# Attention and feed-forward kernel: deeper staging of the weights, 32 halves decoded in 24 units, one more chunk with fp32 value products, feed-forward work from unit 24 on

## The chip, the cores and the metric

The kernel runs on one core of one Trainium2 chip. The metric is the device time of one execution in microseconds (us); of several runs the median is taken. TensorE is called PE here, VectorE DVE, ScalarE ACT, GpSimd POOL and SyncE SP, as in the profile.

## The reference

Attention over 4 batches, 8 heads, 576 positions and head size 64, with a bias from a small network on the distance of two positions, then a layer norm and a feed-forward block of 16 x 128 hidden channels:

```python
scores = scale * np.matmul(q, k.transpose(0, 1, 3, 2))
x = (psi_rel / psi_i)[..., None]
h = np.maximum(x @ w1 + b1, 0.0)
bias = h @ w2
scores = scores + bias.transpose(2, 0, 1)[None, :, :, :]
attn = np.exp(scores - max); attn = attn / (sum + 1e-09)
out = np.matmul(attn, v)
...
xn = (x - mu) / np.sqrt(var + 1e-06) * g_ln
ch = np.maximum(xn @ w_ch1, 0.0) @ w_ch2
return x + ch
```

The feed-forward weights `w_ch1` and `w_ch2` arrive as 64-bit floats, seen by the kernel as pairs of 32-bit words.

## The kernel before, in words

The attention runs in 144 units `(b, c, h)`: batch `b`, a chunk `c` of 128 query rows (chunk 4 is the tail of 64 rows, where a unit takes two heads), head `h`. `ORD` gives the order of the pairs `(b, c)`; units 0 to 7 are the tails of batches 0 and 1, units 8 to 15 chunk 0 of batch 0, 16 to 23 chunk 0 of batch 1, 24 to 39 chunk 0 of batches 2 and 3, 40 to 47 the other two tails, and units of 8 follow to 143. For each unit PE multiplies q and k (`qk`, L390), DVE adds the bias and takes the row maximum (`softmax1`, L414), ACT takes the exponential (L418).

What follows has two forms. Pairs in `NAT` keep fp32: PE transposes the probabilities (`softmax2`, L436 and L437), ACT copies them (L438, L439), and PE multiplies by fp32 v (L486, L503 for the tails). The others split the probabilities into two fp16 parts, on ACT (L423) and DVE (L442, L444), a DMA transposes them (L447, 1152 columns), and PE multiplies by v that is split in two as well (`pv_mms`, L457). For these batches v is measured (`v_max`, L341), the result goes out to DRAM and comes back broadcast (`vall`, reduced at L350), and `split_v` splits it (L365, L368). `uv[b]` is the first unit of batch `b` in the second form; it sets when these steps of the batch are placed.

The feed-forward weights are 32 halves `(f, i)` of 512 KB. `load_w` issues a half on SP's queue into one of two staging buffers (the two slots of `wend`); `decode_w` makes fp32 of it with three DVE instructions (L602, L604, L606), PE adds up a Gram matrix of it (L615), and after 8 halves `w_scale` finds a scale and `split_w` splits each half into fp16 high and low parts (ACT L641, DVE L644) into the slot below. One half is decoded per unit in the program, and each decode is followed by the load of the next half. After a group of 8 halves is split, feed-forward work with it can run: `ffn_micro` does one step, `ffn_w1` (48 matmuls, L667, then ACT L672 and DVE L675 to `hh`) or `ffn_w2` (12 matmuls, L695, into `y`, added to x by DVE L706). There are 144 such steps; a budget `mbank` lets at most two run per unit.

Bias rows are made in 36 groups (`bias_relu`, `bias_mm`), stored to DRAM (`nb`) and loaded skewed, one load per head and chunk (`ldb`), on SP's queue. K, q and v come on POOL's queue. Seven bias groups stand ahead of unit 0; DMAs in `gate` wait for one of them. The program text isn't the last word on order: a scheduler puts each engine's instructions in an order by its own estimate of times, and the engines then run in that order.

Of the kernel before, what the change touches and what calls it, by code (L numbers as in the profile page):

```python
# [22 lines left out]
def kernel(  # L23
# [83 lines left out]
    wslot = [wp.tile([128, 1024], F32, name=f"w{f}") for f in range(NF - 1)]  # L107
# [71 lines left out]
    def bias_mm(gi):  # L179
# [17 lines left out]
        else:  # L197
# [37 lines left out]
    gend = {c: sum(len(range(8 * x, min(36, 8 * x + 8))) for x in corder[:corder.index(c) + 1])  # L235
            for c in range(5)}

    NAT = {(0, 4), (1, 4), (0, 0)}

    def nat_pv(b, c):  # L240
        return (b, c) in NAT

    uv = {}
    for u, (b, c, h) in enumerate(units):
# [4 lines left out]
    seg = []  # L249
    for n, (b, c) in enumerate(ORD):  # L250
        seg.append(seg[-1] + (ORD[n - 1][1] != c) if n else 0)
    loads = []
    for n, (b, c) in enumerate(ORD):
        u0 = ustart[b, c]
        for g in range(4):
            if n == 0 or ORD[n - 1][0] != b:
                loads.append((u0 + (g if c == 4 else 2 * g) - 4, "k", (n, b, g)))
        for hh in range(2 if c < 4 else 1):
            loads.append((u0 + 4 * hh - 3, "q", (b, c, hh)))
        if n == 0 or ORD[n - 1][1] != c:  # L260
            for h in range(NH if c < 4 else 4):
# [11 lines left out]
    gate, gate_on = [], [True]  # L273
# [294 lines left out]

        defer(lo)

    wraw = {}

    def load_w(f, i):
        if f < NF - 2:
            dst = wslot[NF - 1 + i]
        elif f == NF - 2 and i == 1:
            dst = wslot[NF]
        else:
            dst = [ep.tile([128, EW], F32, tag="e", name="wst")[:, 0:512] for _ in range(2)]
            for j in range(2):  # L580
                ld = SY.dma_start(
                    out=dst[j].bitcast(U32),
                    in_=w_ch[f].bitcast(U32)[:, 1024 * i + 512 * j:1024 * i + 512 * j + 512])
                after(ld, ttri[max(ttri)])
            wraw[f, i] = dst
            return
        ld = SY.dma_start(out=dst.bitcast(U32), in_=w_ch[f].bitcast(U32)[:, 1024 * i:1024 * i + 1024])
        if gate_on[0]:
            gate.append((ld, 1 + 2 * i))
        if f >= NF - 2:  # L590
            after(ld, ttri[max(ttri)])
        wraw[f, i] = dst

    def decode_w(f, i):
        wf = wslot[f + 1][:, 512 * i:512 * i + 512]
        src = wraw.pop((f, i))
        src = src if isinstance(src, list) else [src]
        nw = 512 // len(src)
        for j, raw in enumerate(src):
            raw = raw.bitcast(U32).rearrange("p (a b) -> p a b", b=2)  # L600
            w = wslot[f + 1][:, 512 * i + nw * j:512 * i + nw * j + nw].bitcast(U32)
            V.tensor_scalar(out=w, in0=raw[:, :, 1], scalar1=3, scalar2=0x3FFFFFFF,  # L602
                            op0=ALU.logical_shift_left, op1=ALU.bitwise_and)
            V.scalar_tensor_tensor(out=w, in0=raw[:, :, 0], scalar=29, in1=w,  # L604
                                   op0=ALU.logical_shift_right, op1=ALU.bitwise_or)
            V.scalar_tensor_tensor(out=w, in0=raw[:, :, 1], scalar=0xC0000000, in1=w,  # L606
                                   op0=ALU.bitwise_and, op1=ALU.bitwise_or)
        g = GOF[f]
        f0, f1 = GROUPS[g]
        if g not in gram:  # L610
            gram[g] = ps_y.tile([128, 512], F32, tag="y1", name="gram")
        wb = wf.bitcast(BF16).rearrange("p (a b) -> p a b", b=2)[:, :, 1]
        for c in range(4):
            blk = wb[:, 128 * c:128 * c + 128]
            T.matmul(out=gram[g][:, 128 * i:128 * i + 128], lhsT=blk, rhs=blk,  # L615
                     start=(f == f0 and i == 0 and c == 0), stop=(f == f1 - 1 and i == 1 and c == 3))
# [104 lines left out]
    avail_at = []  # L721

    def next_fs(u):
        if not cur_job:
            navail = sum(1 for a in avail_at if a <= u)
            for j in jobs:
                k, g = j
                if blocks[k][-1] < navail and wready_at.get(g, 1 << 30) <= u:
                    jobs.remove(j)
                    nf = 4 // len(blocks[k])  # L730
                    f0, f1 = GROUPS[g]
                    cur_job.extend((k, range(f, f + nf)) for f in range(f0, f1, nf))
                    break
        return cur_job.pop(0) if cur_job else None
# [34 lines left out]
    gate.append((SY.dma_start(out=gs_sb, in_=g_r), 3))  # L769
    wload = [(f, i) for f in range(NF) for i in range(2)]  # L770
    wdec = list(wload)
    for _ in range(2):
        load_w(*wload.pop(0))
    issue_loads(-6)
    V.memset(mhalf, -0.5)
    V.memset(one_sb, 1.0)
    V.memset(half2, 0.5)
    bias_setup()
    issue_loads(-4)
    NP = 7  # L780
# [41 lines left out]
    u = 0  # L822
    while u < NU + 6 or jobs or cur_job or pend or yq:
        if u >= NEARLY:
            ffn_y()
        softmax1(u)
        issue_loads(u)
        softmax2(u - 1)
        flush()
        for _ in range(8):  # L830
            if wdec and 32 - len(wdec) < 1 + (100 * u) // 100:
                f, i = wdec.pop(0)
                decode_w(f, i)
                if i == 1 and f + 1 == GROUPS[GOF[f]][1]:
                    w_scale(GOF[f])
                if wload:
                    load_w(*wload.pop(0))
        while mm_done[0] < ngroup:
            bias_mm(gorder[mm_done[0]])
            mm_done[0] += 1  # L840
        if u % 2:
            qk(u + 1)
            qk(u + 2)
        while npv <= u - LAG:
            if pv(npv):
                lnq.append([u, len(avail_at) + len(lnq)])
            npv += 1
        for fn in todo.pop(u, []):
            fn()
        for g, (f0, f1) in enumerate(GROUPS):  # L850
            if wdone[0] >= 2 * f1 and g not in wready_at:
                wready_at[g] = u
        if u < NU + 9:
            nav = len([a for a in avail_at if a <= u])
            goal = sum(2 * NF * len(bl) // 4 for bl in blocks if bl[-1] < nav)
            nxt = min((steps_av[bl[-1]] for bl in blocks if bl[-1] >= nav), default=NU + 9)
            mbank += max(0.0, (goal - (ntot - nmicro) - mbank)) / max(1, nxt - u)
            mbank = min(mbank, 2.0)
        else:
            mbank = 1.0  # L860
        flush_lo()
        ffn_y()
        while mbank >= 1.0:
            if not ffn_micro(u):
                break
            mbank -= 1.0
            nmicro -= 1
            if mbank >= 1.0:
                ffn_y()
        bneed = NP + 1 + u if u < 8 else 12  # L870
        for c in (1, 2, 3):
            bneed = max(bneed, gend[c] - 8 + min(8, (u - cfirst[c] + 30) * 8 // 26))
        if ngroup < min(36, bneed):
            bias_relu(gorder[ngroup], 1)
            ngroup += 1
        for _ in range(2):
            if wspl:
                split_w(*wspl.pop(0))
        for it in list(lnq):
            if it[0] == u - 1:  # L880
                ln1(it[1])
# [57 lines left out]
```

## Time and profile before

| what | value |
|---|---|
| median of 3 runs | 746.67 us (737.48, 746.67, 750.48) |
| the profiled execution's own time | 743.11 us |
| its span | 741.3 us, so 1.8 us lie outside |
| busy: PE, DVE, ACT, POOL | 651.0, 489.6, 380.9, 87.0 us |
| mean granted clock of PE | 0.929 of full speed |
| moved by DMA | 123.30 MB |

Busy time is the time in which an engine had an instruction running. An average over the span hides that stages have different limits, so the rows below are taken by stage. The first row of each stage is the unit whose L414 begins it.

### The profile page before, as it was taken

The numbers are of one execution on the slowest core, as the hardware profiler recorded it, in microseconds if no ns is written. First come the engines' busy times: TensorE is split into PE (matmuls) and PEld (weight loads), VectorE is DVE, ScalarE is ACT, GpSimd is POOL, SyncE is SP. The second block draws the span as 40 slices with busy tenths as digits, with TensorE's granted clock in tenths as the row PEclk, the third lists the DMA queues.
The fourth block names the chain that finished last, engine by engine and source line by source line (L and its number), as shares of the span: only waits on it lengthen the run. The fifth ranks groups of instructions, "written<-read, shape, count | busy, mean of one in ns | idle before, by whom it ended". The sixth has DMA issues, their size and how long they took to land. (4 is left out here: it accounts for less than half of the span.)

```text
span 741.3 us, 19318 instructions
## 1 busy us (share of the span) xinstructions
PE 651.0 (88%) x7980; PEld 445.9 (60%) x7980; DVE 489.6 (66%) x1114; ACT 380.9 (51%) x731; POOL 87.0 (12%) x160
## 2 busy tenths in 40 slices
PE   4368887576669999999988969999998999999997
PEld 3134465444456766766755647667666767676774
DVE  4467789987788657766585746575675666767322
ACT  4255874453257555556475735566765445454110
POOL 3301120100110010101110101011001101000000
PEclk9668997658969999999999989999999999999999
DMA  7987977699627688977768799686859777646100
GB/s 258 362 241 224 342 239 194 144 234 202 148 61 144 119 154 206 220 153 174 172 107 159 141 191 187 144 178 152 165 118 238 194 150 159 110 81 126 31 16 15
DMA packets 200909, 123.30 MB, mean 166 GB/s; under 512 B 175860, under 2 KB 176116, under 8 KB 200820
## 3 DMA queue, kind: packets, MB, share of 16 engines
q1 hardware_dynamic: 190676, 88.32, 57.0%
q0 software_dynamic: 9280, 33.56, 14.9%
q8 instruction: 63, 1.03, 0.6%
q10 hardware_dynamic: 864, 0.18, 0.2%
q14 instruction: 26, 0.21, 0.1%
HBM read 63.92 MB, written 15.64 MB: 107 GB/s over the span
## 5 line engine op out<-in xcount | busy, mean ns | idle before, releaser
L667 PE MATMUL hps<-xT,w 128*128 128x128 f16 x3240 | 207.1, 225 | 6.9 <-DVE hh L675 3.8
L667 PEld LDWEIGHTS <-w 128*128 128x128 f16 x3240 | 192.4, 101 | 20.2 <-issue 10.2
L418 ACT ACTIVATE t<-t,m 128x576 f32<-128x576 f32 x144 | 111.0, 771 | 179.2 <-DVE m L414 177.7
L695 PE MATMUL y<-w,hh 128*128 128x512 f16 x810 | 190.8, 384 | 1.5 <-DVE x L706 0.8
L442 DVE SCALAR_TENSOR_TENSOR e<-t,e 128x512 f16<-128x512 f32 x128 | 88.2, 689 | 71.4 <-ACT e L423 71.0
L695 PEld LDWEIGHTS <-hh 128*128 128x128 f16 x864 | 80.4, 99 | 89.4 <-issue 4.9
L414 DVE CUSTOM_DVE_ANT_0 t<-sps,ldb 128x576 f32<-128x576 f32 x144 | 107.1, 753 | 25.5 <-PE sps L390 17.4
L390 PE MATMUL sps<-kf,qf 64*128 64x288 f32 (+1 forms) x640 | 104.9, 468 | 8.0 <-DVE m L414 7.8
L457 PE MATMUL xps<-v,pt 128*128 128x64 f16 (+1 forms) x1904 | 79.7, 198 | 31.1 <-DMA pt<-e 26.3
L457 PEld LDWEIGHTS <-pt 128*128 128x128 f16 (+1 forms) x1904 | 66.3, 102 | 64.5 <-issue 32.8
L423 ACT ACTIVATE e<-t 128x576 f16<-128x576 f32 x128 | 86.3, 679 | 12.0 <-DMA pt<-e 9.3
L706 DVE SCALAR_TENSOR_TENSOR x<-y,ycs,x 128x512 f32<-128x512 f32 x72 | 53.9, 749 | 48.3 <-PE y L695 48.1
L672 ACT ACTIVATE hh<-hps 128x512 f16<-128x512 f32 x72 | 42.1, 584 | 69.2 <-PE hps L667 69.2
L390 PEld LDWEIGHTS sps<-kf,qf 64*128 64x128 f32 (+1 forms) x640 | 49.2, 187 | 42.3 <-issue 12.6
L675 DVE SCALAR_TENSOR_TENSOR hh<-hps,hh 128x512 f16<-128x512 f32 x72 | 49.4, 687 | 35.5 <-ACT hh L672 35.1
L291 POOL DMA_DIRECT2D kf<-in_k_s_dram x64 | 36.0, 562 | 262.6 <-PE sps L390 237.8
L172 ACT ACTIVATE r<-psi_sb,pr_sb 128x512 f32<-128x512 f32 (+31 forms) x92 | 52.7, 633 | 6.4 <-DVE pr_sb L123 3.7
L210 PE MATMUL bps<-r,nw_sb 128*32 128x296 f32 (+34 forms) x474 | 34.1, 368 | 11.3 <-DVE r L174 9.9
L602 DVE TENSOR_SCALAR w<-wend 128x512 uint32<-128x512 uint32 x28 | 12.1, 431 | 34.7 <-DMA wend<-in_w_ch_dram 34.7
L304 POOL DMA_DIRECT2D qf<-in_q_main_dram x32 | 17.6, 551 | 120.2 <-PE sps L390 80.0
L210 PEld LDWEIGHTS bps<-r,nw_sb 128*32 128x32 f32 x474 | 16.7, 118 | 21.8 <-issue 10.4
L641 ACT ACTIVATE w<-w,ws 128x512 f16<-128x512 f32 x28 | 19.7, 716 | 17.7 <-DVE ws L113 9.8
(102 smaller groups left out, 548.0 us busy)
## 6 DMA issues: line engine op xcount, KB each, us to landing
kf<-in_k_s_dram POOLq DMA_DIRECT2D x64, 288.0 KB, 4.4
wend<-in_w_ch_dram SPq DMA_DIRECT2D x29, 512.0 KB, 5.7
nb<-ev SPq DMA_DIRECT2D x33, 296.0 KB, 3.6
ldb<-nb SPq DMA_DIRECT2D x32, 288.0 KB, 5.3
qf<-in_q_main_dram POOLq DMA_DIRECT2D x32, 256.0 KB, 4.7
vf<-in_v_p_dram POOLq DMA_DIRECT2D x16, 320.0 KB, 8.0
out_dram<-x SPq DMA_DIRECT2D x18, 256.0 KB, 2.8
ldb<-nb SPq DMA_DIRECT2D x16, 144.0 KB, 8.2
```

The lines of the kernel that those rows point to most:

```text
L172: S.activation(r[:, 0:n], psi_sb[:, 0:n], AF.Relu, bias=pr_sb[:, g4:g4 + 1], scale=1.0)
L210: T.matmul(out=ps[32 * s:32 * s + 32, hf, a - lo:b - lo], lhsT=nw2_sb, rhs=src, start=True, stop=True)
L390: T.matmul(out=o, lhsT=l, rhs=kk, start=True, stop=True, tile_position=(64 * hf, 64 * e))
L414: ttri[u] = V.tensor_tensor_reduce(out=halves(t), in0=ps[:, :, 0:HS], in1=halves(bias), scale=-0.125, scalar=3e38, op0=ALU.add, op1=ALU.mi ...
L418: S.activation(t, t, AF.Exp, bias=m, scale=-1.0, accum_out=l8[b, c][:, h:h + 1])
L423: S.activation(e16[:, 0:SEQ], t, AF.Copy, scale=E_SCALE)
L442: V.scalar_tensor_tensor(out=e16[:, 640:1152], in0=t[:, 0:512], scalar=E_SCALE, in1=e16[:, 0:512], op0=ALU.mult, op1=ALU.subtract)
L457: T.matmul(out=o, lhsT=p[:, m], rhs=v[:, j, a, :], start=(i == 0), stop=(i == len(ops) - 1))
L667: T.matmul(out=h[:, idx * n:idx * n + n], lhsT=w[:, wo + kk * 128:wo + kk * 128 + 128], rhs=xT[k][:, xo + kk, 0:n], start=(i == 0), stop=( ...
L675: V.scalar_tensor_tensor(out=hh[:, 1], in0=h, scalar=0.0, in1=hh[:, 0], op0=ALU.max, op1=ALU.subtract)
L695: T.matmul(out=yps[k][t], lhsT=hh[:, a, o:o + 128], rhs=w[:, wo:wo + 512], start=(f == f0 and i == 0), stop=(f == f1 - 1 and i == 2))
L706: V.scalar_tensor_tensor(out=x, in0=y, scalar=ycs[:, g:g + 1], in1=x, op0=ALU.mult, op1=ALU.add)
```

## The change

Chunk 0 of batch 1 joins `NAT` and is placed ahead of chunk 0 of batch 0. It thus follows the tail of batch 1, whose k is still there: 60 loads of k are issued where there were 64. Units 0 to 23 are then all in the first form, `nat_end` is 24, and `next_fs` starts no feed-forward job in a unit before 24. `uv[1]` moves from unit 16 to unit 64, so v of batch 1 is split late. A half may be staged in any slot that is free, up to six ahead of the decodes; the slots run out towards the end, the last slots staging one half at a time, and the last two halves go through buffers of the pool `e`. The pace in the program is 4 halves in 3 units, from 1 per unit, and a decode and a later load are made to follow the unit's L414.

```diff
-    ORD = [(0, 4), (1, 4), (0, 0), (1, 0), (2, 0), (3, 0), (3, 4), (2, 4),
+    ORD = [(0, 4), (1, 4), (1, 0), (0, 0), (2, 0), (3, 0), (3, 4), (2, 4),
...
-    NAT = {(0, 4), (1, 4), (0, 0)}
+    NAT = {(0, 4), (1, 4), (1, 0), (0, 0)}
...
+    nat_end = max(u for u, (b, c, h) in enumerate(units) if nat_pv(b, c)) + 1
...
-    def load_w(f, i):
-        if f < NF - 2:
-            dst = wslot[NF - 1 + i]
-        elif f == NF - 2 and i == 1:
-            dst = wslot[NF]
+    wraw, decoded = {}, set()
+    stg = {}
+    def load_w():
+        f, i = wload[0]
+        n = 2 * f + i
+        busy = {x for m, x in stg.items() if m not in decoded}
+        fit = [x for x in range(NF + 1) if x not in busy and (2 * x >= n + 3 or x == 0 and n < 6)]
+        if n < 2 * NF - 2:
+            if not fit or n >= len(decoded) + 6:
+                return False
+            stg[n] = fit[0]
+            dst = wslot[fit[0]]
         else:
+            if n >= len(decoded) + 2:
+                return False
             dst = [ep.tile([128, EW], F32, tag="e", name="wst")[:, 0:512] for _ in range(2)]
...
+            if gate_on[0]:
+                gate.append((ld, min(NP - 1, n + 1)))
+            else:
                 after(ld, ttri[max(ttri)])
...
+            if ttri:
+                after(dec, ttri[max(ttri)])
...
     def next_fs(u):
+        if u < nat_end:
+            return None
...
-    for _ in range(2):
-        load_w(*wload.pop(0))
+    NP = 7
+    while load_w():
+        pass
...
-            if wdec and 32 - len(wdec) < 1 + (100 * u) // 100:
+            if wdec and 32 - len(wdec) < 1 + (4 * u) // 3:
...
-                if wload:
-                    load_w(*wload.pop(0))
+                while wload and load_w():
+                    pass
```

On SP's queue, ahead of the first bias load of unit 0 (`ldb`), three loads of weight halves (`in_w_ch_dram`) stand between the stores of bias groups (`nb`) before:

```order
L220 DMA nb4_133<-ev_238 16x8x592
L587 DMA wend_153<-in_w_ch_dram 128x1024
L220 DMA nb4_133<-rp_262 16x8x592
L220 DMA nb4_133<-ev_286 16x8x592
L769 DMA gs_sb_119<-in_g_r_dram 128x512
L587 DMA wend_153<-in_w_ch_dram 128x1024
L220 DMA nb4_133<-ev_310 16x8x592
L220 DMA nb0_129<-rp_334 16x8x592
L220 DMA nb0_129<-ev_358 16x8x592
L587 DMA wend_153<-in_w_ch_dram 128x1024
L220 DMA nb0_129<-rp_374 16x8x592
L326 DMA ldb_384<-nb4_133 64x576
```

The same stretch of SP's queue after the change, from the second weight load on (one more stands ahead of these rows):

```order
L594 DMA w2_140<-in_w_ch_dram 128x1024
L220 DMA nb4_133<-ev_290 16x8x592
L783 DMA gs_sb_119<-in_g_r_dram 128x512
L594 DMA w3_141<-in_w_ch_dram 128x1024
L220 DMA nb4_133<-ev_314 16x8x592
L594 DMA w4_142<-in_w_ch_dram 128x1024
L220 DMA nb0_129<-rp_338 16x8x592
L594 DMA w5_143<-in_w_ch_dram 128x1024
L220 DMA nb0_129<-ev_362 16x8x592
L594 DMA w6_144<-in_w_ch_dram 128x1024
L220 DMA nb0_129<-rp_378 16x8x592
L328 DMA ldb_388<-nb4_133 64x576
```

Six weight loads now stand ahead of the first bias load, where three did, and they go to six different slots.

DVE at unit 20 before (L442 and L444 make the low fp16 part of the probabilities, L368 that of v, L341 measures v, L675 makes `hh`, L604 is the second decode instruction, always out of `wend`):

```order
L442 SCALAR_TENSOR_TENSOR e_1420<-t,e_1420 128x512
L444 SCALAR_TENSOR_TENSOR e_1420<-t,e_1420 128x64
L368 SCALAR_TENSOR_TENSOR v<-vf,vs,v 128x10x64
L113 TENSOR_SCALAR vs<-var 128x4
L414 ISA t,m<-sps,ldb 128x576
L414 ISA m 128x1
L341 TENSOR_REDUCE vam<-vf 128x1
L675 SCALAR_TENSOR_TENSOR hh<-hps,hh 128x512
L604 SCALAR_TENSOR_TENSOR w_147<-wend,w_147 128x512
L442 SCALAR_TENSOR_TENSOR e_1461<-t,e_1461 128x512
L444 SCALAR_TENSOR_TENSOR e_1461<-t,e_1461 128x64
```

DVE around the same unit after the change (L612, L616 and L618 are the three decode instructions, now out of slots `w_149` to `w_152`):

```order
L416 ISA t,m<-sps,ldb 128x576
L416 ISA m 128x1
L612 TENSOR_SCALAR w_147<-w_149 128x512
L612 TENSOR_SCALAR w_147<-w_150 128x512
L612 TENSOR_SCALAR w_148<-w_151 128x512
L612 TENSOR_SCALAR w_148<-w_152 128x512
L416 ISA t,m<-sps,ldb 128x576
L416 ISA m 128x1
L112 TENSOR_SCALAR var<-var 128x4
L616 SCALAR_TENSOR_TENSOR w_147<-w_149,w_147 128x512
L616 SCALAR_TENSOR_TENSOR w_147<-w_150,w_147 128x512
```

The splitting of the probabilities and the feed-forward work are gone from these units, and four halves are begun together, each out of a buffer of its own.

## Rows read from the trace of the kernel before

**Rows 1.** Windows: busy us of each engine, granted clock, DMA share, GB/s.
```profile
20.00:42.30 22.30, 6.01 (x56) 2.54 (x52) 11.05 (x23) 4.20 (x6) 5.96 (x11) 0.60 1.02 350
42.30:85.70 43.40, 35.63 (x443) 20.87 (x443) 30.85 (x72) 29.25 (x59) 5.20 (x9) 0.85 0.81 250
85.70:149.40 63.70, 47.80 (x397) 32.88 (x395) 56.84 (x128) 38.34 (x80) 11.13 (x21) 0.82 0.75 211
149.40:218.00 68.60, 46.20 (x460) 31.81 (x461) 54.98 (x130) 28.94 (x51) 8.19 (x11) 0.72 0.75 167
218.00:294.80 76.80, 76.80 (x1048) 51.76 (x1047) 52.44 (x122) 45.83 (x85) 6.23 (x11) 0.99 0.75 147
...
80.00:100.00 20.00, 16.33 (x181) 11.13 (x178) 16.48 (x39) 16.29 (x36) 3.04 (x6) 1.00 0.91 323
...
370.00:380.00 10.00, 7.29 (x87) 4.98 (x83) 8.96 (x20) 7.47 (x14) 1.38 (x3) 1.00 0.48 92
```

**Rows 2.** Timeline of DVE: L414 of units 0, 8, 24, 32 and 48.
```profile
42.33 0.76 DVE L414 CUSTOM_DVE_ANT_0 t<-sps,ldb 128x576 f32<-128x576 f32 x1 [0.95 <-DMA ldb<-nb]
...
85.72 0.75 DVE L414 CUSTOM_DVE_ANT_0 t<-sps,ldb 128x576 f32<-128x576 f32 x1
...
149.38 0.75 DVE L414 CUSTOM_DVE_ANT_0 t<-sps,ldb 128x576 f32<-128x576 f32 x1
...
218.01 0.75 DVE L414 CUSTOM_DVE_ANT_0 t<-sps,ldb 128x576 f32<-128x576 f32 x1
...
294.82 0.76 DVE L414 CUSTOM_DVE_ANT_0 t<-sps,ldb 128x576 f32<-128x576 f32 x1 [0.37 <-DMA ldb<-nb]
```

**Rows 3.** Waits of DVE from 42.3, from 149.4, from 350: us, times, longest.
```profile
DVE w L602 <- DMA wend<-in_w_ch_dram: 15.7, 7, 5.3
...
DVE w L602 <- DMA wend<-in_w_ch_dram: 8.5, 6, 2.3
DVE x L706 <- PE y L695: 4.3, 2, 2.3
...
DVE var L350 <- DMA vall<-vmx: 4.4, 1, 4.4
```

**Rows 4.** The chain that ended last: two steps of feed-forward work.
```profile
696.80 2.68 PE hps L667 x48
699.48 2.59 PE y L695 x12
```

**Rows 5.** DMA issues by line: KB each, median us from issue to landing.
```profile
wend<-in_w_ch_dram SPq DMA_DIRECT2D x29, 512.0 KB, 5.7
```

**Rows 6.** Groups of instructions on DVE, whole span: count, busy us, mean ns.
```profile
L442 DVE SCALAR_TENSOR_TENSOR e<-t,e 128x512 f16<-128x512 f32 x128 | 88.2, 689 | 71.4 <-ACT e L423 71.0
...
L706 DVE SCALAR_TENSOR_TENSOR x<-y,ycs,x 128x512 f32<-128x512 f32 x72 | 53.9, 749 | 48.3 <-PE y L695 48.1
...
L675 DVE SCALAR_TENSOR_TENSOR hh<-hps,hh 128x512 f16<-128x512 f32 x72 | 49.4, 687 | 35.5 <-ACT hh L672 35.1
...
L444 DVE SCALAR_TENSOR_TENSOR e<-t,e 128x64 f16<-128x64 f32 x128 | 28.0, 218 | 0.0
...
L604 DVE SCALAR_TENSOR_TENSOR w<-wend,w 128x512 uint32<-128x512 uint32 x28 | 19.2, 687 | 0.2
L606 DVE SCALAR_TENSOR_TENSOR w<-wend,w 128x512 uint32<-128x512 uint32 x28 | 19.2, 687 | 0.2
...
L368 DVE SCALAR_TENSOR_TENSOR v<-vf,vs,v 128x640 f16<-128x640 f32 x16 | 14.0, 874 | 0.2 <-ACT v L365 0.2
...
L341 DVE TENSOR_REDUCE vam<-vf 128x1 f32<-128x640 f32 x16 | 12.5, 811 | 0.0
...
L602 DVE TENSOR_SCALAR w<-wend 128x512 uint32<-128x512 uint32 x28 | 12.1, 431 | 34.7 <-DMA wend<-in_w_ch_dram 34.7
```

**Rows 7.** Timeline of PE in units 8 to 15: transposes, three units apart.
```profile
95.22 0.66 PE L436 MATMUL ptm<-id_sb,t 128*128 128x128 f32 x4
...
103.42 0.66 PE L436 MATMUL ptm<-id_sb,t 128*128 128x128 f32 x4
```

More of the change, by code (lines that the diff above doesn't have):

```diff
@@ L569, in ln2 @@
         defer(lo)
-    wraw = {}
-    def load_w(f, i):
-        if f < NF - 2:
-            dst = wslot[NF - 1 + i]
-        elif f == NF - 2 and i == 1:
-            dst = wslot[NF]
-        else:
+    wraw, decoded = {}, set()
[10 more added lines that the diff above has]
+            dst = wslot[fit[0]]
+        else:
+            if n >= len(decoded) + 2:
+                return False
             dst = [ep.tile([128, EW], F32, tag="e", name="wst")[:, 0:512] for _ in range(2)]
[L580 to L583, printed above, removed]
-                after(ld, ttri[max(ttri)])
[L585 to L591, printed above, removed]
+        wload.pop(0)
+        for j, d in enumerate(dst if isinstance(dst, list) else [dst]):
+            w = d.shape[1]
+            ld = SY.dma_start(out=d.bitcast(U32),
+                              in_=w_ch[f].bitcast(U32)[:, 1024 * i + w * j:1024 * i + w * j + w])
+            if gate_on[0]:
+                gate.append((ld, min(NP - 1, n + 1)))
+            else:
+                after(ld, ttri[max(ttri)])
         wraw[f, i] = dst
+        return True
     def decode_w(f, i):
@@ L596, in decode_w @@
         src = wraw.pop((f, i))
+        decoded.add(2 * f + i)
         src = src if isinstance(src, list) else [src]
@@ L601, in decode_w @@
             w = wslot[f + 1][:, 512 * i + nw * j:512 * i + nw * j + nw].bitcast(U32)
-            V.tensor_scalar(out=w, in0=raw[:, :, 1], scalar1=3, scalar2=0x3FFFFFFF,
-                            op0=ALU.logical_shift_left, op1=ALU.bitwise_and)
+            dec = V.tensor_scalar(out=w, in0=raw[:, :, 1], scalar1=3, scalar2=0x3FFFFFFF,
+                                  op0=ALU.logical_shift_left, op1=ALU.bitwise_and)
+            if ttri:
+                after(dec, ttri[max(ttri)])
             V.scalar_tensor_tensor(out=w, in0=raw[:, :, 0], scalar=29, in1=w,
@@ L779 @@
     issue_loads(-4)
-    NP = 7
     for n in range(NP + 1):
```

## The prediction

> **What bounds the kernel now.** I read the windows by stage first [rows 1]. From 218 us on PE is busy without a gap (76.80 of 76.80 us, granted clock 0.99); what PE has left to do then sets the end. Ahead of that it isn't: from 149.4 to 218.0 PE is busy for 46.20 of 68.60 us at a clock of 0.72, while DVE is busy for 54.98. The marks by unit [rows 2] give the stages: unit 0 begins on DVE at 42.33, unit 8 at 85.72, unit 24 at 149.38, unit 32 at 218.01, unit 48 at 294.82. So the question is when DVE reaches unit 32, and how much feed-forward work PE then owes.
>
> From unit 0 to unit 32 175.7 us go by. DVE is busy in 30.85 + 56.84 + 54.98 = 142.7 of them [rows 1] and idle in 33.0. The waits name the largest cause [rows 3]: the first decode instruction stands for a weight half that has not landed, 15.7 us up to 149.4 and 8.5 us from there to 218. That is 24.2 us; DVE runs in order, so the next L414 is behind each of these waits. The other 8.8 us have several causes, 4.3 of them a wait for y of PE.
>
> **The start.** Unit 0 waits for its bias rows (0.95 us idle until ldb landed) [rows 2]. From 20 to 42.3 us the DMA engines are full: share 1.02 at 350 GB/s [rows 1]. Three more weight halves of 512 KB [rows 5] now stand ahead of those rows on SP's queue; at 350 GB/s one takes 1.5 us, three 4.5 us. Four loads of v move ahead of two of k on POOL's queue as well, which I bound at two more us in the same full stretch and at nothing if they fall behind. I take 4.5: unit 0 at 46.8 us, bounds 42.3 and 48.8.
>
> The Trainium skill says in DMA: Bandwidth & Descriptors, section Issuing engines are not separate DMA queues, that transfers from SP, ACT and POOL end up on the same 16 engines and interleave, so that another queue saves only issue time. By that rule POOL's extra loads count like SP's, and unit 0 would begin at 48.8 and the end come 2 us later than my sum; the share of 1.02 agrees with a common limit, but no row shows what lies ahead of what.
>
> **DVE's work up to unit 32.** I counted the instructions between the L414 of unit 0 and that of unit 32 in both orders and priced the differences [rows 6]. A whole decode is 0.431 + 0.687 + 0.687 = 1.81 us: 30 stand there now, 26 before (before, three were done ahead of unit 0, now none): +7.2. Two half-sized decodes fewer, at half of that each: -1.8. Two more L341 of 0.811: +1.6. Four L368 of 0.874 move to units past 60: -3.5. Eight splits of probabilities go (0.689 + 0.218): -7.3. One hh (0.687) and two y (0.749) fewer: -2.2. The sum is -6.0: 136.7 us of DVE work in place of 142.7. So most of the gain can't come from less work, it must come from the waits.
>
> **The waits for weights.** With up to six halves ahead and one decode per 136.7/32 = 4.3 us of DVE work, a half is asked for some 26 us ahead; landing takes 5.7 us in the median [rows 5]. That leaves nothing of the waits as long as slots are free. They run out for halves 28 and 29, which use one slot in turn: in DVE's order 16 and 8 instructions lie between the end of the decode ahead and the next decode, at some 0.46 us an instruction (136.7 us by their count of 299) 7.4 and 3.7 us, against 5.7 for the landing. I take 2 us for what is left; bounds 0 and 8.5, the sum of the same stretch before. The wait of a decode or a load for L414 is free on DVE, where the order has it so anyway; on SP a load that waits there holds up what is behind it, but up to unit 23 these are bias rows asked for seven units early and no transposes of probabilities.
>
> Unit 32 thus comes at 46.8 + 136.7 + 8.8 + 2.0 = 194.3 us instead of 218.0: 23.7 us earlier.
>
> **What comes back.** In DVE's order 8 feed-forward results (hh and y) stand ahead of unit 32 before, 5 now; ahead of unit 48 it is 29 and 30. So PE has 25 steps to do between these units instead of 21. A step is 2.68 or 2.59 us [rows 4], and PE is full there [rows 1]: 4 x 2.64 = +10.5 us. From unit 48 on the order is the old one, one step ahead: -2.6. The fp32 form costs PE more in units 16 to 23, but DVE covers it: three such units take 103.42 - 95.22 = 8.2 us of PE [rows 7], 2.7 each, at full clock, against 56.84 us of DVE for 16 units [rows 1], 3.6 each. If that cover goes it is the third rival. And v of batch 1 is now scaled in the full stretch: for batch 0 this step made DVE wait 4.4 us for `vall` [rows 3], and in the 10 us behind it PE stood for 10 - 7.29 = 2.7 us [rows 1]. A second one, near unit 57: +2.7 (bounds 0 and 4.4). Fewer DMAs (4 loads of k, 8 transposes) I count at nothing: behind 218 us DMA is not what PE waits for, but for short stalls, and ahead of unit 24 they only ease the start's queue.
>
> The sum: -23.7 + 10.5 - 2.6 + 2.7 = -13.1 us, a span of 728.2 and with 1.8 us outside **730 us**. The profiled run's 743.1 is 3.6 us under the median of 746.67, so this is -1.8% against the one and -2.2% against the other; 2% is about what a measurement of this kernel can tell from no change.
>
> **Rivals.** (1) The waits move rather than go: the front is bound by DMA, unit 0 is late by 6.5 us and half of the wait for weights stays (12.1 us), since the share is 0.75 to 0.81 all the way [rows 1]. Unit 32 at 48.8 + 136.7 + 8.8 + 12.1 = 206.4, 11.6 earlier; 743.1 - 11.6 + 10.5 - 2.6 + 2.7 = **742**. This is also the case that the change does little of what it says: by the order both kernels have all halves decoded only by unit 32. For it speaks the full DMA at the start; against it that the load of a half was always begun only after a decode. (2) The better end: unit 0 at 42.3, no wait for weights, the other waits halved (4.4), no stall at `vall`: unit 32 at 183.4, and 743.1 - 34.6 + 10.5 - 2.6 = **716**. (3) The slower side: PE goes cold in units 8 to 23. Without feed-forward steps PE has only fp32 units there; the granted clock is 0.60 from 20 to 42 us, where PE is busy for 6.01 of 22.30 us [rows 1]. At the lower level of 1.2 GHz a unit takes PE 5.4 us instead of 2.7, 16 of them 87 us, against 57 us in my sum: +30 and **760**. It decides once the granted clock is under 2.7/3.6 = 0.75. Against it: from 80 to 100 us, in just such units, the clock was 1.00 with PE busy for 16.33 of 20 us [rows 1].
>
> The Trainium skill, TensorE: Matmul & The Clock Gate, section What's actually happening, has the throttled state as the default that activity releases; by that rule alone the sparser PE of units 8 to 23 speaks for the third rival, and the row from 80 to 100 us speaks against it.
>
> **How the numbers follow.** I give the forecast 0.50 (722 to 738), the first rival 0.27, the second 0.15, the third 0.08. The range must leave out at most 0.2: from 714, past the second rival, to 750, past the first with its bounds; the third stays outside. Faster by over 2% is under 731.7: all of the second rival, somewhat over half of the forecast, little else: 0.47. Slower by over 2% is over 761.6: most of the third and a tail of the first: 0.08. Within 2%: 0.45.
>
> **What would show it.** Right: DVE's wait for weights from unit 0 to unit 32 falls from 24.2 us to some 2, unit 0 at 45 to 49 us, unit 32 near 194, PE without a gap from there, unit 48 near 281, and a second stall near unit 57. Wrong: unit 32 after 206 (the waits went elsewhere: ldb, or the PE clock in units 8 to 23), or PE with gaps between units 32 and 48, so that the steps owed cost more than 10.5 us, or new waits for transposes past unit 80, which would be a different order of DMAs and no term of this sum.

## The result, and the profile after

| what | before | changed |
|---|---|---|
| median of 4 runs each | 745.17 us (737.48 to 750.48) | 724.81 us (715.63 to 730.36) |
| the profiled execution: time, span | 743.11, 741.3 us | 726.42, 724.6 us |
| busy: PE, DVE, ACT, POOL | 651.0, 489.6, 380.9, 87.0 us | 645.3, 480.1, 382.8, 86.5 us |
| mean granted clock of PE | 0.929 | 0.955 |
| moved by DMA | 123.30 MB | 119.76 MB |

The ratio is 0.969 with a 95% interval of 0.962 to 0.976. A later measurement of both (run e9_changed_again, below) gave medians of 744.67 and 722.96 and a ratio of 0.981 (0.974 to 0.988). The changed kernel is faster in both, by 2 to 3%; that it is over 2% the later measurement does not show. Ratios are taken without disturbed runs (in the later measurement five of the 17 runs of the kernel before are left), medians over all of them, and the profiles of the changed kernel, e1, e7, e8 and e12 are of such disturbed runs.

The profile of the later measurement (span 720.8 us) has the stages that follow here within 1 us each up to unit 48, and within 2 us behind it.

Lines have moved: L416 of the changed kernel is L414 of before, L392 is L390, L612 to L618 are the decode, L594 is the load of a half. The marks of units 0, 8, 24, 32 and 48 in the timeline of DVE of the changed kernel (start, duration, then what the engine had stood idle for), which answer to [rows 2]:

```profile
50.74 0.76 DVE L416 CUSTOM_DVE_ANT_0 t<-sps,ldb 128x576 f32<-128x576 f32 x1 [13.58 <-DMA ldb<-nb]
...
91.06 0.76 DVE L416 CUSTOM_DVE_ANT_0 t<-sps,ldb 128x576 f32<-128x576 f32 x1 [0.83 <-PE ptl L439]
...
146.96 0.74 DVE L416 CUSTOM_DVE_ANT_0 t<-sps,ldb 128x576 f32<-128x576 f32 x1
...
192.56 0.75 DVE L416 CUSTOM_DVE_ANT_0 t<-sps,ldb 128x576 f32<-128x576 f32 x1
...
282.67 0.75 DVE L416 CUSTOM_DVE_ANT_0 t<-sps,ldb 128x576 f32<-128x576 f32 x1
```

Unit 0 is 8.4 us late against before, unit 8 still 5.3; by unit 24 the changed kernel is 2.4 us ahead, by unit 32 25.5, and by unit 48 12.1. The windows of the changed kernel between marks (units 0 to 8, 8 to 16, 16 to 24, 24 to 32, 32 to 48, the rest), with the columns of [rows 1]:

```profile
50.74:91.06 40.32, 31.08 (x435) 19.40 (x436) 37.43 (x78) 28.21 (x57) 2.95 (x5) 0.86 0.67 200
91.06:112.87 21.81, 20.29 (x188) 15.11 (x189) 21.62 (x49) 17.70 (x40) 4.86 (x8) 1.00 1.03 377
112.87:146.96 34.09, 29.30 (x214) 22.56 (x213) 32.27 (x77) 19.91 (x45) 6.41 (x9) 0.90 0.67 179
146.96:192.56 45.60, 36.83 (x395) 26.54 (x394) 43.70 (x107) 27.27 (x50) 7.33 (x9) 0.85 0.65 148
192.56:282.67 90.11, 89.22 (x1202) 60.82 (x1201) 55.91 (x129) 47.31 (x88) 7.45 (x13) 1.00 0.63 126
282.67:724.60 441.93, 425.53 (x5384) 295.55 (x5378) 274.99 (x621) 228.84 (x443) 41.11 (x79) 0.99 0.76 144
```

From unit 0 to unit 32 DVE is now busy in 37.43 + 21.62 + 32.27 + 43.70 = 135.0 of 141.8 us; before it was 142.7 of 175.7. From unit 32 on PE is full, as before, but units 32 to 48 take 90.1 us where they took 76.8. The waits of DVE in the changed kernel from 50.7 to 192.6 us (total, times, longest), which answer to [rows 3]:

```profile
DVE t L416 <- DMA ldb<-nb: 13.6, 1, 13.6
DVE wend L612 <- DMA wend<-in_w_ch_dram: 1.9, 2, 1.0
DVE r L174 <- DMA nb<-ev: 1.6, 1, 1.6
DVE w L612 <- DMA w<-in_w_ch_dram: 1.1, 1, 1.1
```

The first line is the idle time that ends with unit 0's mark, and so lies ahead of the stretch. The waits for weights are 1.9 + 1.1 = 3.0 us; they were 24.2. At the start, the DMA issues of the changed kernel from 14 to 36 us (issues, KB each, median us from issue to landing) show what unit 0 stood behind:

```profile
w<-in_w_ch_dram SPq DMA_DIRECT2D x6, 512.0 KB, 16.2
```

These are the six halves ahead of unit 0, issued from 16.8 to 29.2 us. One takes 16.2 us in the median (12.7 in the later measurement), against 7.0 for the four halves that the kernel before issues up to 42 us, and 5.7 over its whole span [rows 5].

### The profile page after: what moved, and what is told of

Same layout as the page of the kernel before. It is cut to its first block, busy times and chain, and to the rows that moved or that the text cites. A ratio compares the mean times of both kernels' runs of the same rounds, so it can differ in the third digit from the quotient of the medians.

```text
span 724.6 us, 19301 instructions
## 1 busy us (share of the span) xinstructions
PE 645.3 (89%) x7988; PEld 447.4 (62%) x7988; DVE 480.1 (66%) x1095; ACT 382.8 (53%) x739; POOL 86.5 (12%) x156
## 2 busy tenths in 40 slices
DMA packets 190973, 119.76 MB, mean 165 GB/s; under 512 B 166308, under 2 KB 166564, under 8 KB 190884
## 3 DMA queue, kind: packets, MB, share of 16 engines
q0 software_dynamic: 8960, 32.38, 14.8%
## 5 line engine op out<-in xcount | busy, mean ns | idle before, releaser
L679 PE MATMUL hps<-xT,w 128*128 128x128 f16 x3240 | 197.8, 221 | 3.5 <-DVE hh L687 2.1
L707 PE MATMUL y<-w,hh 128*128 128x512 f16 x810 | 191.8, 386 | 1.0 <-DVE x L718 0.8
L679 PEld LDWEIGHTS <-w 128*128 128x128 f16 x3240 | 185.7, 99 | 9.2 <-issue 3.5
L707 PEld LDWEIGHTS <-hh 128*128 128x128 f16 x864 | 81.1, 99 | 90.1 <-issue 7.9
L444 DVE SCALAR_TENSOR_TENSOR e<-t,e 128x512 f16<-128x512 f32 x120 | 82.6, 689 | 77.4 <-ACT e L425 77.2
L416 DVE CUSTOM_DVE_ANT_0 t<-sps,ldb 128x576 f32<-128x576 f32 x144 | 106.6, 750 | 25.6 <-DMA ldb<-nb 13.8
L392 PE MATMUL sps<-kf,qf 64*128 64x288 f32 (+1 forms) x640 | 100.7, 439 | 4.5 <-DVE m L416 3.8
L459 PEld LDWEIGHTS <-pt 128*128 128x128 f16 (+1 forms) x1792 | 61.8, 100 | 57.6 <-issue 31.8
L425 ACT ACTIVATE e<-t 128x576 f16<-128x576 f32 x120 | 79.4, 677 | 15.5 <-DMA pt<-e 13.4
L459 PE MATMUL xps<-v,pt 128*128 128x64 f16 (+1 forms) x1792 | 73.9, 195 | 12.2 <-DMA pt<-e 11.5
L718 DVE SCALAR_TENSOR_TENSOR x<-y,ycs,x 128x512 f32<-128x512 f32 x72 | 53.7, 746 | 19.5 <-PE y L707 19.5
L392 PEld LDWEIGHTS sps<-kf,qf 64*128 64x128 f32 (+1 forms) x640 | 48.6, 177 | 28.4 <-issue 7.3
L210 PE MATMUL bps<-r,nw_sb 128*32 128x296 f32 (+33 forms) x474 | 33.7, 364 | 34.1 <-DVE r L174 28.4
L210 PEld LDWEIGHTS bps<-r,nw_sb 128*32 128x32 f32 x474 | 16.2, 117 | 45.0 <-issue 30.8
L546 POOL TENSOR_SCALAR rs<-mv 128x1 f32<-128x1 f32 x18 | 8.7, 484 | 173.6 <-DVE mv L545 142.4
L420 ACT ACTIVATION_READ_ACCUMULATOR t<-t,m 128x1 f32 x144 | 27.0, 187 | 0.0
## 6 DMA issues: line engine op xcount, KB each, us to landing
qf<-in_q_main_dram POOLq DMA_DIRECT2D x32, 256.0 KB, 4.6
out_dram<-x SPq DMA_DIRECT2D x18, 256.0 KB, 2.5
```

The lines of the kernel that those rows point to most:

```text
L210: T.matmul(out=ps[32 * s:32 * s + 32, hf, a - lo:b - lo], lhsT=nw2_sb, rhs=src, start=True, stop=True)
L392: T.matmul(out=o, lhsT=l, rhs=kk, start=True, stop=True, tile_position=(64 * hf, 64 * e))
L416: ttri[u] = V.tensor_tensor_reduce(out=halves(t), in0=ps[:, :, 0:HS], in1=halves(bias), scale=-0.125, scalar=3e38, op0=ALU.add, op1=ALU.mi ...
L420: S.activation(t, t, AF.Exp, bias=m, scale=-1.0, accum_out=l8[b, c][:, h:h + 1])
L425: S.activation(e16[:, 0:SEQ], t, AF.Copy, scale=E_SCALE)
L444: V.scalar_tensor_tensor(out=e16[:, 640:1152], in0=t[:, 0:512], scalar=E_SCALE, in1=e16[:, 0:512], op0=ALU.mult, op1=ALU.subtract)
```

## The experiments

Marks, in us, of each kernel's profiled execution, and the median of its runs. "Done" counts the feed-forward results on DVE (`hh` + `y`) ahead of the mark; the median of the kernel before in the same session is in the last column.

| kernel | unit 0 | unit 32 | done | unit 48 | done | from unit 48 on | median | before |
|---|---|---|---|---|---|---|---|---|
| before | 42.3 | 218.0 | 4+4 | 294.8 | 15+14 | 446.5 | 745.2 | |
| changed | 50.7 | 192.6 | 3+2 | 282.7 | 16+14 | 441.9 | 724.8 | 745.2 |
| e1_depth2 | 38.3 | 204.5 | 3+2 | 295.0 | 16+14 | 441.3 | 732.1 | 743.7 |
| e2_start2 | 38.7 | 188.7 | 2+2 | 287.7 | 16+14 | 437.4 | 731.1 | 743.7 |
| e3_staging_only | 44.6 | 211.0 | 5+4 | 287.6 | 15+14 | 443.8 | 735.3 | 743.7 |
| e4_fp32_only | 46.7 | 200.3 | 5+4 | 276.9 | 15+14 | 445.4 | 728.5 | 743.7 |
| e5_pace1 | 48.2 | 194.7 | 4+3 | 276.9 | 15+14 | 443.8 | 728.2 | 737.4 |
| e6_before_noload | 42.5 | 186.0 | 6+5 | 256.0 | 15+14 | 451.6 | 706.2 | 737.4 |
| e7_late_v | 43.8 | 195.6 | 3+2 | 287.0 | 16+14 | 447.7 | 727.8 | 737.4 |
| e8_late_v_start3 | 38.2 | 196.8 | 3+2 | 287.5 | 16+14 | 441.6 | 722.3 | 737.4 |
| e9_changed_again | 48.4 | 190.7 | 3+2 | 280.8 | 16+14 | 440.0 | 723.0 | 744.7 |
| e10_fp32_again | 44.1 | 200.7 | 5+4 | 278.2 | 15+14 | 452.1 | 733.9 | 744.7 |
| e11_pace1_again | 48.9 | 198.2 | 4+3 | 276.6 | 15+14 | 440.7 | 728.3 | 744.7 |
| e12_combo | 38.4 | 191.8 | 4+3 | 275.1 | 15+14 | 449.1 | 721.8 | 744.7 |

The runs of one kernel lie up to 21 us apart (e11_pace1_again: 716.8 to 738.3), so a difference of 5 us between two medians of four to twelve runs settles nothing; the marks are read for the mechanism and the ratios for the size.

**Is it the depth of the staging?** The changed kernel with at most two halves ahead (e1_depth2), and with two until unit 0 and six later (e2_start2):

```diff
-            if not fit or n >= len(decoded) + 6:
+            if not fit or n >= len(decoded) + 2:
```

> The changed kernel with at most two halves ahead of the decodes instead of six; the rest of the change stays. Weights theory (the gain is the decode's wait for a half that has not landed): unit 0 starts earlier, at 43 to 46 us, but some 20 us of waits for weights come back by unit 32, which comes at 205 to 215 us, and the time is 735 to 745 us. Rival (the gain is the work and the DMAs that the fp32 form takes away, and the front free of feed-forward steps): the time stays at 718 to 728 us.

```diff
-            if not fit or n >= len(decoded) + 6:
+            if not fit or n >= len(decoded) + (2 if gate_on[0] else 6):
```

> The changed kernel with two halves ahead until the first bias groups are stored and six from unit 0 on. If the late start of unit 0 (50.7 against 42.3 us) is the price of six weight halves ahead of the bias rows: unit 0 at 43 to 46 us, everything behind it as much earlier, 716 to 720 us. Rival: the first decodes then wait for weights as before and eat the earlier start, unit 8 stays at 91 us and the time at 722 to 727 us.

With two ahead all the way the ratio is 0.977 (0.966 to 0.988), between the two expectations. DVE's waits from 38.3 to 204.5 us in e1_depth2:

```profile
DVE t L416 <- DMA ldb<-nb: 10.4, 2, 10.0
DVE w L612 <- DMA w<-in_w_ch_dram: 6.1, 4, 2.1
...
DVE w L612 <- DMA wend<-in_w_ch_dram: 0.9, 1, 0.9
DVE wend L612 <- DMA wend<-in_w_ch_dram: 0.9, 1, 0.9
```

In the first line 10.0 us are the idle time that ends with unit 0's mark. Two halves ahead leave 6.1 + 0.9 + 0.9 = 7.9 us of waiting for weights, not 24.2. So most of those waits go without the depth. Unit 0 begins at 38.3 us, 12.4 earlier than with six halves, yet unit 32 comes 11.9 later: DVE idles for 166.2 - 138.2 = 28.0 us in between, of which 15.9 are waits for PE.

With the depth restored behind unit 0 (e2_start2) the ratio is 0.984 (0.976 to 0.992): no gain over the changed kernel, though unit 0 is again 12 us early and unit 32 3.9 us early. Of the rival expectation only the outcome held, that the earlier start is lost: what is saved ahead of unit 0 is not found at unit 48 (287.7 against 282.7). It isn't lost where it said, for unit 8 comes at 81.1 us, not 91, and no decode waits for weights ahead of unit 16; and 731.1 us is over both stated ranges.

**Which half of the change carries it?** Staging alone: the changed kernel with `ORD`, `NAT`, the hold on feed-forward work and the pace as before. The fp32 form alone: the kernel before with the new `ORD`, `NAT` and hold, still on two buffers.

```diff
-    ORD = [(0, 4), (1, 4), (1, 0), (0, 0), (2, 0), (3, 0), (3, 4), (2, 4),
+    ORD = [(0, 4), (1, 4), (0, 0), (1, 0), (2, 0), (3, 0), (3, 4), (2, 4),
...
-    NAT = {(0, 4), (1, 4), (1, 0), (0, 0)}
+    NAT = {(0, 4), (1, 4), (0, 0)}
...
-        if u < nat_end:
-            return None
...
-            if wdec and 32 - len(wdec) < 1 + (4 * u) // 3:
+            if wdec and 32 - len(wdec) < 1 + u:
```

> The kernel before with the deeper staging alone: old order, old NAT, no hold on feed-forward steps, one decode per unit. Weights theory: waits for weights from unit 0 to unit 32 fall from 24 to under 5 us, unit 0 is late as in the changed kernel (49 to 52 us), unit 32 at 200 to 208 us, 727 to 735 us. Rival (fp32 form and free front): no more than the waits shift, 740 to 747 us.

```diff
-    ORD = [(0, 4), (1, 4), (0, 0), (1, 0), (2, 0), (3, 0), (3, 4), (2, 4),
+    ORD = [(0, 4), (1, 4), (1, 0), (0, 0), (2, 0), (3, 0), (3, 4), (2, 4),
...
-    NAT = {(0, 4), (1, 4), (0, 0)}
+    NAT = {(0, 4), (1, 4), (1, 0), (0, 0)}
...
     def next_fs(u):
+        if u < nat_end:
+            return None
```

> The kernel before with chunk 0 of batch 1 in fp32, the exchanged order and no feed-forward step before unit 24, on the old staging of two halves and the old pace. Weights theory: DVE still waits some 24 us for weights up to unit 32, which comes at 207 to 214 us; the steps held back and the second scaling of v in the full stretch take back most of it, 738 to 748 us. Rival: this is the change that pays, 722 to 730 us.

Staging alone gives 0.986 (0.981 to 0.992), the fp32 form alone 0.980 (0.972 to 0.988). DVE's waits in e3_staging_only from 44.6 to 211.0 us:

```profile
DVE t L416 <- DMA ldb<-nb: 7.5, 1, 7.5
DVE var L352 <- DMA vall<-vmx: 6.4, 2, 5.8
DVE r L174 <- DMA nb<-ev: 4.2, 3, 2.3
DVE w L612 <- DMA wend<-in_w_ch_dram: 1.7, 2, 1.5
DVE wend L612 <- DMA wend<-in_w_ch_dram: 1.5, 1, 1.5
```

The first line is again the idle time ahead of unit 0's mark. The waits for weights fall to 3.2 us, as in the changed kernel, but DVE still idles 166.4 - 146.9 = 19.5 us between units 0 and 32: waits for `vall` and for stores of bias rows (`nb`), 0.2 us before, come to 10.6. That is the first rival's mechanism, though it had the waits for weights stay. DVE's work there also grows by 4.2 us, and unit 32 is only 7.0 us earlier than before.

The fp32 form alone, on two buffers, moves unit 32 by 17.7 us: DVE's work falls from 142.7 to 135.1 us and its idle time from 33.0 to 18.5, while unit 0 is 4.4 late. Its wait for weights in e4_fp32_only from 46.7 to 200.3 us, which was 24.2 us before:

```profile
DVE w L604 <- DMA wend<-in_w_ch_dram: 9.8, 9, 2.0
```

The program loads each half into the same two buffers as before, but the halves land sooner. The kernel before from 42.3 to 218 us (issues by tile, median us to landing):

```profile
wend<-in_w_ch_dram SPq DMA_DIRECT2D x25, 512.0 KB, 5.7
...
pt<-e SPq DMA_TRANSPOSE x16, 6.8
```

The same from 46.7 to 200.3 us in e4_fp32_only:

```profile
wend<-in_w_ch_dram SPq DMA_DIRECT2D x25, 512.0 KB, 4.2
...
pt<-e SPq DMA_TRANSPOSE x8, 4.9
```

Eight transposes of probabilities, four loads of k, four of v and one of `vall` are gone from the stretch, and the 25 halves land in 4.2 instead of 5.7 us (4.3 in the repeat). Which of the removed transfers does it was not taken apart, and that it is the landing alone is not shown either. By stage (units 0 to 8, 8 to 16, 16 to 24, 24 to 32) the waits for weights were 9.6, 1.1, 5.0 and 8.5 us, and are 5.5, 2.0, 0 and 2.2 (5.9, 1.6, 0.5 and 4.9 in the repeat). The transposes that are gone belonged to units 16 to 24, where 5.0 us of waits go (4.5 in the repeat); but 4.1 and 6.3 us (3.7 and 3.6) go in the first and the last stage, where 2 loads of k are issued instead of 6, and 8 transposes instead of 10.

**What are the waits for weights worth in all?** The kernel before, with the halves behind the first two and ahead of the last four not loaded:

```diff
     def load_w(f, i):
+        if 0 < f < NF - 2:
+            wraw[f, i] = wslot[NF - 1 + i]
+            return
```

> The kernel before, but 26 of its 32 weight halves are not loaded: their decodes read what the two staging buffers hold from the first loads, so that the weights are wrong and 13.6 MB less is moved. It bounds what the waits for weights and their DMAs are worth. Weights theory: the 24.2 us of waits from unit 0 to unit 32 are gone and nothing takes their place, 150 to 155 us from unit 0 to unit 32 instead of 175.7, 718 to 728 us. Rival (the waits only stand where DVE would wait for transposes, bias rows or PE anyway): 165 us or more, 733 to 742 us.

The ratio is 0.955 (0.947 to 0.963), better than expected. Windows of e6_before_noload, units 0 to 32 and 32 to 48:

```profile
42.50:186.00 143.50, 119.82 (x1354) 80.97 (x1355) 130.07 (x304) 96.22 (x189) 22.87 (x39) 0.89 0.63 154
...
186.02:256.03 70.01, 69.81 (x999) 47.16 (x998) 51.53 (x122) 44.32 (x84) 7.29 (x13) 1.00 0.76 161
```

Units 0 to 32 take 143.5 us instead of 175.7. Not all of that is waiting: DVE idles for 13.4 us instead of 33.0, and its work falls from 142.7 to 130.1 because decodes that wait for nothing run earlier (18.6 us of them ahead of unit 0, where there were 5.5). What was gained at unit 32 (32.0 us) is still there at unit 48 (38.8 us), since more feed-forward results, not fewer, stand ahead of unit 32 (6+5). The other transfers of the stretch land sooner too: a transpose in 3.9 us (6.8 before), a load of k in 3.8 (5.7). So the loads of weights lengthen the others here; e4_fp32_only speaks for the converse.

**Does the start set unit 32?** The changed kernel with v of batches 2 and 3 loaded behind the mark of the unit that asks for it (e7_late_v), and this with three halves at the start (e8_late_v_start3):

```diff
                 if gate_on[0] and key[0]:
                     gate.append((ld, 3))
+                elif ttri:
+                    after(ld, ttri[max(ttri)])
```

> The changed kernel with v of batches 2 and 3 loaded only behind the L414 of the unit that asks for it, from unit 5 on, instead of ahead of unit 0. If the DMAs that stand ahead of the bias rows set the start: eight loads of 320 KB leave a stretch that moved 384 GB/s, 6.8 us, unit 0 at 43 to 46 us instead of 50.7, 716 to 721 us. Rival: the loads then delay later ones (k, bias rows of units 8 on) as much, 722 to 730 us.

```diff
-            if not fit or n >= len(decoded) + 6:
+            if not fit or n >= len(decoded) + (3 if gate_on[0] else 6):
```

> As e7, and three halves of the weights instead of six ahead of the bias rows. With both away from the start: unit 0 at 38 to 41 us, no wait of 10 us for bias rows at unit 2, unit 8 at 75 to 80 us, 712 to 718 us. Rival, as the run with two halves ahead showed: the wait moves to units 2 to 20, unit 24 not under 145 us, 722 to 732 us.

Ratios 0.983 (0.974 to 0.992) and 0.975 (0.965 to 0.985). Unit 0 moves to 43.8 and 38.2 us, unit 32 to 195.6 and 196.8, later than in the changed kernel. Units 16 to 24 hold the difference. e8_late_v_start3 there:

```profile
104.35:152.56 48.21, 36.90 (x195) 29.28 (x194) 41.93 (x93) 20.72 (x44) 10.21 (x13) 0.61 0.78 163
```

e4_fp32_only there:

```profile
115.50:138.99 23.49, 21.89 (x175) 17.28 (x175) 23.49 (x58) 16.65 (x37) 6.40 (x8) 1.00 0.61 203
```

The same eight fp32 units take 48.2 us at a granted clock of 0.61 and 23.5 us at 1.00; the changed kernel lies between (34.1 us at 0.90), e2_start2 at 43.8 us and 0.68, e7_late_v at 41.4 us and 0.71 (one execution each). That is the third rival's stage with its clock under 0.75, met by the kernels that start early. PE is busy 15 us longer for nearly the same matmuls (x195 and x175), but it isn't PE that DVE waits for. DVE's waits in e8_late_v_start3 from 104.35 to 152.56 us, and the line that measures v there (L345, L343 in the changed kernel):

```profile
DVE vam L345 <- DMA vf<-in_v_p_dram: 3.0, 1, 3.0
DVE w L614 <- DMA wend<-in_w_ch_dram: 1.9, 1, 1.9
DVE w L614 <- DMA w<-in_w_ch_dram: 1.4, 1, 1.4
...
L345 DVE TENSOR_REDUCE vam<-vf 128x1 f32<-128x640 f32 x12 | 9.0, 808 | 3.0 <-DMA vf<-in_v_p_dram 3.0
```

Of the 48.2 us DVE is busy for 41.9 and idle for 6.3, all of them for loads; in e12_combo (below) it is busy for 39.4 of the 39.6 us of these units, at a clock of 0.75. So DVE's work and its loads set this stage, and the slower clock cost no wait there. Of the kernels that start early only e1_depth2 shows DVE waiting for PE in these units, 2.9 us at a clock of 0.71. Of the 18.4 us of DVE work that e8_late_v_start3 has there beyond e4_fp32_only (41.93 against 23.49), 9.0 are the twelve measurings of v, which the late load itself moves here (in the changed kernel 14 of them stand in units 0 to 8), and 7.5 are decodes.

Over units 0 to 32 DVE's work is nearly the same in these kernels, and the earlier start comes back as its idle time: 6.8 us in the changed kernel, 14.0 in e2_start2, 14.2 in e7_late_v, 21.1 in e8_late_v_start3 and 15.0 in e12_combo, with 135.0 to 138.3 us of work in all five.

**The pace, and a combination.** The changed kernel at one decode per unit (e5_pace1), this repeated with the changed kernel and the fp32 form alone on one chip (e9 to e11), and pace, late v and three halves together (e12_combo, the edits of e5 and e8):

```diff
-            if wdec and 32 - len(wdec) < 1 + (4 * u) // 3:
+            if wdec and 32 - len(wdec) < 1 + u:
```

> The changed kernel at the old pace of one decode per unit; staging, fp32 form and hold stay. If the pace only shifts DVE's work (the same decodes up to unit 32): unit 24 some 9 us earlier, unit 32 as in the changed kernel, 720 to 730 us. Rival (the pace is what the fp32 form alone lacks, 0.980 against 0.969): later groups of weights hold up the first feed-forward steps, unit 48 comes 5 to 10 us later, 730 to 736 us.

> The changed kernel itself, on the same chip and in the same rounds as the next three. 722 to 728 us, 0.965 to 0.975 of the kernel before.

> The fp32 form, the exchanged order and the hold alone, beside the changed kernel. If deeper staging and pace add what the prediction says (waits for weights from 9.8 to 3 us, some 7 us, less the late start): 4 to 8 us more than the changed kernel. Rival (they add nothing once the fp32 form has shortened the landing of a half): within 2 us of it.

> The changed kernel at one decode per unit, beside the changed kernel. If the pace only shifts DVE's work: within 3 us of it. If the pace carries part of the gain: 4 us or more slower.

> One decode per unit, v of batches 2 and 3 loaded from unit 5 on, three halves of the weights ahead of the bias rows and six later. If an earlier start reaches unit 32 at this pace: unit 0 at 38 to 42 us, unit 32 at 186 to 190 us, 4 to 8 us faster than the changed kernel. Rival (the start is not what sets unit 32): unit 32 at 193 to 198 us and within 3 us of the changed kernel.

e5_pace1 measured 0.984 (0.977 to 0.992) in its session; in the common session the medians are 722.96 (changed), 733.91 (fp32 form alone), 728.25 (pace 1) and 721.80 (combination), with ratios of 0.981 (0.974 to 0.988), 0.993 (0.987 to 0.999), none that could be taken, and 0.977 (0.966 to 0.987). The pace stays unsettled: its runs (716.8 to 738.3) cover those of the changed kernel (721.3 to 737.9). The two runs at the old pace are also the staging of e3 and the fp32 form of e4 together: with the same 15+14 done they reach unit 48 at 276.9 and 276.6 us, the fp32 form alone at 276.9 and 278.2, staging alone at 287.6. Up to there staging adds nothing to the fp32 form that the marks show. The combination starts at 38.4 us, 10 earlier, and ends within 2 us of the changed kernel: the rival's side, though unit 32, at 191.8 us, lies in neither stated range.

The changed kernel against the fp32 form alone is the sharper case. The medians say 4 and 11 us for staging and pace. The marks do not show where up to unit 48: the fp32 form alone reaches it at 276.9 and 278.2 us, the changed kernel at 282.7 and 280.8, with one `hh` more done, a step of 2.68 us [rows 4]. Less that, it is 280.0 and 278.2. Windows of e4_fp32_only, units 24 to 32, 32 to 48 and the rest:

```profile
138.99:200.33 61.34, 52.38 (x528) 38.67 (x529) 53.39 (x127) 31.17 (x58) 6.04 (x11) 0.83 0.73 164
200.33:276.87 76.54, 76.54 (x1039) 52.05 (x1038) 52.04 (x122) 45.16 (x85) 6.44 (x11) 0.98 0.72 140
276.87:722.30 445.43, 428.41 (x5436) 299.44 (x5432) 278.26 (x622) 228.00 (x444) 41.98 (x79) 0.98 0.70 144
```

The changed kernel is 7.7 us ahead at unit 32, but with 3+2 results done instead of 5+4; its next stage takes 90.1 us instead of 76.5, which gives the lead back. Behind unit 48 PE's idle time decides between single profiles: 17.0 us in e4_fp32_only, 21.3 in its repeat (the same program), 16.4 in both profiles of the changed kernel.

The hold on feed-forward work was not undone by itself: the fp32 transposes and the feed-forward steps use the same PSUM buffers, and that was not tried.

## Why the prediction was right, and where it was not

The time, 724.8 us, lies in the range and 5 us under the forecast of 730; the side (faster by over 2%) was the likelier of the two that held most of the chance, by 0.47 to 0.45. Term by term, in us of the profiled execution:

| term | forecast | measured |
|---|---|---|
| unit 0 begins | 46.8 | 50.7 |
| DVE's work from unit 0 to unit 32 | 136.7 | 135.0 |
| waits for weights | 2.0 | 3.0 |
| other waits | 8.8 | 3.8 |
| unit 32 begins | 194.3 | 192.6 |
| units 32 to 48 | 87.3 | 90.1 |
| unit 48 begins | 281.6 | 282.7 |
| from unit 48 on | 446.6 | 441.9 |
| span | 728.2 | 724.6 |

That the span came within 4 us was in part luck: the start (+3.9) and units 32 to 48 (+2.8) cost more than forecast, the other waits (-5.0) and the part behind unit 48 (-4.7) less, for reasons that the prediction did not give. Of the other waits, the 4.3 us for y of PE are gone from the changed kernel's list; the prediction had kept them.

**What held.** DVE's idle time ahead of unit 32 was the place: it falls from 33.0 to 6.8 us, and to 13.4 in the kernel before without the loads (e6_before_noload). The count of DVE instructions with their durations came within 1.7 us, the waits for weights within 1, and the four owed steps were paid as PE's time behind unit 32, 13.3 us where 10.5 were set down.

**The start was mis-sized, and did not add.** Unit 0 came at 50.7 us, outside the bounds of 42.3 to 48.8, and at 48.4 in the later measurement, inside them. Three halves at 350 GB/s were priced at 1.5 us each. From e2_start2 and e1_depth2 (two halves, v as in the changed kernel, unit 0 at 38.7 and 38.3) to the changed kernel (six, 50.7 and 48.4) four more cost 9.7 to 12.4 us, 2.4 to 3.1 each. And taking v of batches 2 and 3 out of the start brings unit 0 from 50.7 and 48.4 to 43.8 us with all six halves kept. The Trainium skill, DMA: Bandwidth & Descriptors, section Issuing engines are not separate DMA queues, has transfers of all issuing engines interleave on the same 16 DMA engines; this step agrees, since transfers issued by POOL held back rows issued by SP, and 48.8, the time by that rule, was nearer than my 46.8. As a term of the sum, though, the +4.5 fails: with unit 0 anywhere from 38.2 to 50.7 us and up to six halves ahead behind it, unit 32 came between 188.7 and 198.2, in no order with unit 0, and an earlier start came back as idle time of DVE.

**"Fewer DMAs I count at nothing" was the wrong step.** The prediction gave the fall of the waits for weights (24.2 to 2.0) to the deeper staging. The fp32 form alone takes them to 9.8 (12.9 in the repeat) on the old two buffers, where the halves land in 4.2 us instead of 5.7, and two halves ahead in the changed kernel leave 7.9. Staging alone takes away more of them (3.2 are left), but brings other DMA waits up (19.5 us of idle time stay). At unit 32 the two seem to add: 7.0 + 17.7 = 24.7 us against 25.5 for both; but each alone has 5+4 results done there, both together 3+2. At unit 48 they don't add: 7.2 and 17.9 alone, 12.1 together, or 14.8 at equal feed-forward work, and 17.9 and 18.2 together at the old pace. So the forecast had the right waits, but put at nothing the part that most of the gain up to unit 48 comes with.

**Behind unit 48** the second stall for `vall` (+2.7) did not reach PE: at unit 57 DVE waits for it for 1.0 us, and PE is busy for all of the 10 us around it (320 to 330 us). PE's work fell by 428.5 - 425.5 = 3.0 us, as the step set down at 2.6 should make it. PE's idle time went from 18.0 to 16.4 us, where the forecast had it grow by 2.7; that 4.3 us is most of the 4.7 by which this part was too long. The window of the kernel before for it, to set against the last row of the changed kernel's windows above:

```profile
294.82:741.30 446.48, 428.52 (x5434) 299.49 (x5432) 273.98 (x613) 224.91 (x440) 42.02 (x79) 0.98 0.69 142
```

As PE's idle time there differs by 4.3 us between two profiles of the fp32 form alone, this last gain is not claimed for the change.

**The rivals.** The first (the waits move) is what staging alone does, at 735 us where the rival said 742; the fp32 form spared the whole change from it. The second's end, 716, was not reached: its early start can be had, but returns nothing. The third did not occur in the changed kernel (clock 1.00 and 0.90 in units 8 to 24). In its variants with an early start the clock did fall to 0.61 to 0.75 in units 16 to 24, but DVE waited for PE there for 2.9 us at most, so that the 30 us of this rival were not paid.

No kernel here that loads all its weights clearly beats the changed one: the combination's 721.8 us and the 722.3 of e8_late_v_start3 lie within the scatter of its 723.0 and 724.8.

## What to carry to other kernels

A wait for a load has two cures, more buffers and fewer transfers beside it; before the gain is put down to the first, ask what the change takes off the DMA engines in the same stretch, since the fp32 form on two buffers took as much of DVE's idle time (33.0 to 18.5 us) as six buffers alone (to 19.5). A mark that comes earlier is worth only what has been done by then: compare marks at equal work on the engine that is full afterwards, as the units from 32 to 48 paid back 13 of 25 us. And a term for a late start is not added to the sum until the trace shows that the next stage follows it.

## What the runs showed of the hardware

- The landing time of one and the same plain load of 512 KB from DRAM was 4.2, 5.7 and 16.2 us in the median, by what else was under way (units 0 to 32 of e4_fp32_only and of the kernel before, and the changed kernel's start); a transpose of probabilities took 3.9, 4.9 and 6.8 us in units 0 to 32 with, in turn, most of the weight loads, half of the transposes, or none of either taken away (e6, e4, before).
- The granted clock of PE in the same eight fp32 units (16 to 24) was 1.00, 0.90, 0.75, 0.71, 0.68 and 0.61 in kernels that differ in when transfers, decodes and the measuring of v fall (e4, changed, e12, e7, e2, e8); at 0.61 PE took 36.9 us for 195 matmuls, at 1.00 21.9 us for 175. In none of these six does the trace show DVE waiting for PE in these units: PE was busy for 15 us more, and the stage's length was set elsewhere.
- One program's time from unit 48 on was 445.4 and 452.1 us in two profiles of the fp32 form alone, 4.3 of these 6.7 us in PE's idle time. A single profile can't tell a change of 5 us there.
